# Start of an attention + FFN kernel: first 512 tokens of q and k in two token stages instead of two head halves

## The chip, the cores and the metric

The kernel runs on one core of one Trainium2 chip. The metric is the device time of one execution in microseconds (us), so lower is better. Times inside a trace are counted from the start of the span. "Granted clock" is the clock that the throttle gave the matrix engine, as a share of full speed; the mean over an execution is listed for every run.

The engines are called as in the profile: PE (matmuls and transposes), PEld (its weight loads), DVE (vector engine), ACT (scalar engine), POOL (GpSimd) and SP. A letter q behind a name, as in SPq, means the queue that the engine issues DMAs to. POOLq is served by software and is called the software queue below; SPq and ACTq are hardware queues.

## The reference

```python
# q, k, v: (8, 8, 576, 64) float32: 8 sequences, 8 heads, 576 tokens, head size 64
scores = q @ k.T / sqrt(64)                        # per sequence and head
mask   = (0 <= qpos - kpos) & (qpos - kpos < 64)   # causal window of 64
attn   = softmax(where(mask, scores, -1e9))
x      = (attn @ v).reshape(4608, 512)             # tokens x (heads * 64)
g      = x @ w_gate                                # w_gate, w_val: (512, 1536)
y      = (g * sigmoid(g) * (x @ w_val)) @ w_out    # w_out: (1536, 512)
```

The output is 4608 x 512 float32. Inside, the kernel works in bf16.

## The kernel before

The kernel walks over 36 tiles of 128 tokens. For each tile it transposes q and k (step T), computes scores and exponentials (Sx), multiplies with v and normalises (AV), and transposes the result to xT (X). Four tiles make one FFN block of 512 tokens: twelve steps F (gate and value matmuls for 128 of the 1536 hidden columns each, followed by a tanh on ACT and two operations, uu and hT, on DVE), then the output matmuls. Attention of later tiles is woven between FFN steps, so that PE always has work once the first block runs. The matter is the start, before the first FFN block is under way.

The first 512 tokens of q and k come in four loads, two per tensor, each for four heads. In each load a partition takes four adjacent tokens of a head, 4 x 64 floats, so one run of memory is 1 KB:

```python
def first_loads(self):
    for half in range(2):
        hs = slice(4 * half, 4 * half + 4)
        for eng, dst, src, nm in (("sp", self.fk, self.k, "fk"), ("act", self.fq, self.q, "fq")):
            d = dst[:, hs].rearrange("p h j d -> p h (j d)")
            a = src[0, hs, 0:512, :].rearrange("h (p j) d -> p h (j d)", j=4)
            self.g.op(eng, lambda e, d=d, a=a: e.dma_start(d, a), writes=[(nm, half)], dma=True)
```

All other loads of the start go through the software queue in the order in which they are issued. The order of the start, cut to what matters:

```python
self.first_loads()
self.load_v(0, False)                  # software queue from here
...
for n in range(1, 4):
    self.load_v(n, False)
W(0, 1); W(1, 2)                       # first columns of both FFN weights
...
for f in range(2, 12, 2):
    W(f, f + 2)
...                                    # warm-up matmuls, first casts and transposes
self.Sx(0, 0, True)                    # scores: heads 0-3 of tiles 0-3, then heads 4-7
self.Sx(1, 0, True)
self.first_T("q", 1)
self.Sx(2, 0, True)
self.Sx(3, 0, True)
self.AV(0, 0)
self.Sx(0, 1, True)
...
self.X(1, "act")
self.AV(3, 0)
self.AV(3, 1)
self.F2(0, 0)                          # FFN steps 0 and 1, tokens 0-255
self.X(2, "act")
self.X(3, "act")
self.F2(0, 1)                          # FFN steps 0 and 1, tokens 256-511
load(4)                                # tile 4: q, k, v, behind all W in the queue
load(5)
...
for f in range(2, 6):
    self.F(0, f)
self.T(4)                              # transposes of tile 4, then kT copy on DVE, qz copies on ACT
self.F(0, 6)
self.Sx(4, 0)
self.F(0, 7)
...
```

In T, the copy of k (kT) on DVE must run before the two copies of q (qz) on ACT, and only then can the scores of the tile start.

The softmax here doesn't subtract the row's maximum and nothing guards it: scores larger than these inputs give would overflow.

## Time and profile before

| what | before |
|---|---|
| time, median of 3 runs (lowest to highest) | 350.63 us (350.61 to 350.97) |
| span of the trace, mean granted clock | 348.8 us, 1.0 |
| PE busy | 335.0 us, 96% |
| last of the four first loads lands | 9.67 us |
| v of tile 0 lands | 10.20 us |
| first FFN matmul | 20.86 us |
| FFN step 4 starts | 29.77 us |
| k of tile 4 lands | 33.06 us |
| scores of tile 4 start | 36.23 us |

The first line shown is the busy time of each engine, from the page of the kernel before (busy us, share of the span, number of instructions):

```profile
PE 335.0 (96%) x2385; PEld 175.4 (50%) x2385; DVE 220.4 (63%) x461; ACT 149.2 (43%) x252; POOL 127.3 (37%) x176
```

PE is the engine that bounds the kernel. What is left to win without taking work off PE is its idle time, and that lies mostly at the start. The table of stretches of the kernel before shows it (columns: stretch and its length; busy us and instructions of PE, PEld, DVE, ACT, POOL; granted clock; busy DMA share; GB/s):

```profile
15.00:20.00 5.00, 4.29 (x96) 4.04 (x96) 3.34 (x13) 3.39 (x7) 5.00 (x10) 1.00 1.37 229
20.00:25.00 5.00, 3.19 (x31) 2.58 (x32) 1.28 (x5) 1.28 (x4) 5.00 (x8) 1.00 1.45 196
```

The timeline of PE in the kernel before names the waits (start, busy us, engine, line, operation, out<-in, shape, count, and in brackets the idle time just before and what ended it):

```profile
20.86 0.61 PE L564 MATMUL ps<-xT,Wg 128*128 128x256 bf16 x4 [0.88 <-DVE xb L494]
24.29 0.61 PE L564 MATMUL ps<-xT,Wg 128*128 128x256 bf16 x4 [0.95 <-ACT xT L515]
...
33.23 0.39 PE L411 MATMUL ps<-ident,kn 128*128 128x128 bf16 x4
...
36.23 0.40 PE L454 MATMUL ps<-qz,kT 128*128 128x128 bf16 x4 [0.67 <-ACT qz L419]
```

PE waits 0.88 us for the last normalised attention output before the first FFN half step and 0.95 us for xT before the second halves. The transposes of tile 4 then start at 33.23 us, and its scores wait for a chain that the view of the critical chain spells out (start, length, what):

```profile
33.19 0.70 DVE uu L546
...
33.92 0.69 DVE hT L548
34.61 0.35 DVE kT L416
...
34.98 0.59 ACT qz L417
...
36.23 0.40 PE ps L454 x4
```

The kT copy of tile 4 stands behind hT of FFN step 5 on DVE and so starts at 34.6 us, although its transposes end about 33.8 us. Thus two things hold tile 4 back: DVE's queue, and a DMA, because k of tile 4 lands only at 33.06 us. The view of DMA issues of the kernel before shows the loads of the start and those of tile 4 (out<-in, queue, count, KB each, median us from issue to landing):

```profile
f<-in_k_dram SPq DMA_DIRECT2D x2, 512.0 KB, 6.4
va<-in_v_dram POOLq DMA_DIRECT2D x1, 128.0 KB, 8.9
...
kn<-in_k_dram POOLq DMA_DIRECT2D x2, 64.0 KB, 12.8
```

A load of 64 KB that takes 12.8 us is not slow itself: it stands in the software queue behind weights.

### The profile page before, as it was taken

What the parts mean: (1) busy time and instruction counts of PE and PEld (TensorE: products, weight loads), DVE (VectorE), ACT (ScalarE), POOL (GpSimd) and SP (SyncE); (2) the same over time, 40 slices, a digit from 0 to 9 for tenths busy, and PEclk for the clock granted to TensorE, in tenths of its full rate; (3) what the DMA queues carried; (4) which work ended last, traced back from release to release, by engine and by line L of the source; (5) the groups of instructions that cost most, each with busy time, mean ns of one, the idle gap of its engine ahead of it and who ended that gap; (6) DMA issues with size and microseconds to landing.
All of it is one profiled execution on the core that took longest, in us unless ns stands there. A gap on an engine that the chain in (4) does not pass through costs nothing.

```text
span 348.8 us, 6255 instructions
## 1 busy us (share of the span) xinstructions
PE 335.0 (96%) x2385; PEld 175.4 (50%) x2385; DVE 220.4 (63%) x461; ACT 149.2 (43%) x252; POOL 127.3 (37%) x176
## 2 busy tenths in 40 slices
PE   8779889999999999999999999999999999999996
PEld 3654445554555545555555555555555555444444
DVE  7848583477966665666666666666666666655520
ACT  3643746765544444444444444444444444232321
POOL 8997726835633318233324445334100000000000
PEclk9999999999999999999999999999999999999999
DMA  8999999999989999999999999999945511100012
GB/s 242 188 204 171 218 157 209 201 146 181 141 63 162 148 166 135 150 155 173 137 154 161 169 142 151 159 169 141 160 112 131 94 55 48 59 32 30 30 45 107
DMA packets 177949, 47.93 MB, mean 137 GB/s; under 512 B 160128, under 2 KB 173440, under 8 KB 177920
## 3 DMA queue, kind: packets, MB, share of 16 engines
q0 software_dynamic: 113584, 17.84, 71.4%
q1 hardware_dynamic: 63136, 28.52, 39.8%
q10 hardware_dynamic: 1200, 1.18, 1.0%
q8 instruction: 19, 0.31, 0.4%
q14 instruction: 10, 0.08, 0.1%
HBM read 37.75 MB, written 9.44 MB: 135 GB/s over the span
## 4 chain that ended last, share of the span: by engine, by line
PE 79%; DVE 12%; ACT 5%; DMA 2%; issue 1%
PE ps L538 45%; PE ps L597 23%; PE ps L454 4%; DVE hT L548 3%; DVE uu L546 2%; PE ps L485 2%; PE ps L484 2%; PE ps L357 2%; DMA xT<-xb 2%; DVE xb L494 2%; DVE pt L472 1%; ACT sig L544 1%; ACT qz L419 1%; ACT qz L417 1%; PE ps L564 1%
## 5 line engine op out<-in xcount | busy, mean ns | idle before, releaser
L546 DVE SCALAR_TENSOR_TENSOR uu<-sig,ps 128x512 bf16<-128x512 bf16 x106 | 72.5, 684 | 92.5 <-ACT sig L544 92.2
L538 PE MATMUL ps<-xT,Wg 128*128 128x512 bf16 x424 | 108.8, 379 | 1.0 <-DMA xT<-xb 0.8
L538 PE MATMUL ps<-xT,Wv 128*128 128x512 bf16 x424 | 108.8, 379 | 0.0
L597 PE MATMUL ps<-Wo,hT 128*128 128x512 bf16 x420 | 96.2, 379 | 0.6 <-DVE hT L548 0.6
L544 ACT ACTIVATE sig<-ps 128x512 bf16<-128x512 f32 x106 | 63.3, 597 | 61.5 <-PE ps L538 61.4
L548 DVE SCALAR_TENSOR_TENSOR hT<-uu,ps 128x512 bf16<-128x512 bf16 x106 | 72.8, 686 | 3.7
L538 PEld LDWEIGHTS ps<-xT,Wv 128*128 128x128 bf16 x424 | 41.5, 98 | 50.0 <-DVE hT L583 0.2
L597 PEld LDWEIGHTS ps<-Wo,hT 128*128 128x128 bf16 x420 | 39.8, 98 | 43.5 <-DVE hT L548 0.7
L466 ACT ACTIVATE pt<-ps 128x512 bf16<-128x512 f32 x72 | 42.5, 597 | 43.3 <-PE ps L454 43.2
L538 PEld LDWEIGHTS ps<-xT,Wg 128*128 128x128 bf16 x424 | 39.4, 98 | 41.9 <-DMA xT<-xb 1.3
L371 POOL DMA_DIRECT2D va<-in_v_dram x40 | 34.1, 859 | 66.9 <-PE ps L454 64.9
L288 POOL DMA_DIRECT2D qd<-in_q_dram x54 | 39.0, 734 | 31.6 <-DMA qz<-qd 31.6
L609 ACT ACTIVATE ost<-ps 128x512 f32<-128x512 f32 x35 | 20.9, 597 | 67.1 <-PE ps L597 67.1
L288 POOL DMA_DIRECT2D kn<-in_k_dram x36 | 31.0, 868 | 12.3 <-PE ps L411 11.3
L494 DVE TENSOR_TENSOR xb<-ps,rc 128x256 bf16<-128x256 f32 x72 | 30.5, 424 | 2.5
L454 PE MATMUL ps<-qz,kT 128*128 128x128 bf16 x288 | 28.8, 219 | 3.3 <-ACT qz L419 2.1
L472 DVE TENSOR_TENSOR pt<-pt,mask 128x512 bf16<-128x512 bf16 x64 | 26.6, 415 | 6.3 <-ACT pt L466 6.2
L484 PE MATMUL ps<-vb,pt 128*128 128x65 bf16 x288 | 25.8, 193 | 0.1
L485 PE MATMUL ps<-va,pt 128*128 128x65 bf16 x288 | 25.9, 193 | 0.0
L484 PEld LDWEIGHTS ps<-vb,pt 128*128 128x128 bf16 x288 | 22.0, 98 | 6.7 <-DVE pt L472 0.3
L485 PEld LDWEIGHTS ps<-va,pt 128*128 128x128 bf16 x288 | 19.8, 98 | 6.4
L454 PEld LDWEIGHTS ps<-qz,kT 128*128 128x128 bf16 x288 | 18.7, 97 | 6.6 <-ACT qz L419 3.1
(64 smaller groups left out, 135.1 us busy)
## 6 DMA issues: line engine op xcount, KB each, us to landing
out_dram<-ost SPq DMA_DIRECT2D x35, 256.0 KB, 3.3
vb<-va SPq DMA_DIRECT2D x68, 80.0 KB, 3.4
va<-in_v_dram POOLq DMA_DIRECT2D x32, 128.0 KB, 5.2
kn<-in_k_dram POOLq DMA_DIRECT2D x28, 128.0 KB, 5.8
qd<-in_q_dram POOLq DMA_DIRECT2D x42, 64.0 KB, 4.1
Wo<-in_moe_w_out_dram POOLq DMA_DIRECT2D x2, 768.0 KB, 17.6
Wg<-in_moe_w_gate_dram POOLq DMA_DIRECT2D x5, 256.0 KB, 11.0
Wv<-in_moe_w_val_dram POOLq DMA_DIRECT2D x5, 256.0 KB, 11.6
```

The lines of the kernel that those rows point to most:

```text
L288: self.g.op("pool", lambda e, d=d, a=az: e.dma_start(d, a), writes=kz, dma=True)
L371: g.op("pool", lambda e, d=d, a=a: e.dma_start(d, a), writes=ks, dma=True)
L454: r = e.matmul(sv[:, w, c], self.kT[:, pr, k0:k0 + 128], qz[:, pr, :, 64 * w:64 * w + 64], start=not bias, stop=True)
L466: g.op("act", lambda e: e.activation(po, si, ACTF.Exp, scale=SCALE), reads=[bk], writes=[pk])
L484: e.matmul(av[:, j, :], pt[:, h, 0:128], vb[:, h, 0:65], start=True, stop=False)
L485: r = e.matmul(av[:, j, :], pt[:, h, 64:192], va[:, h, 0:65], start=False, stop=True)
L494: g.op("dve", lambda e: e.tensor_tensor(xo, av[:, :, 0:64], rb, ALU.mult), reads=[bk, ("rc", ir)], writes=[("xb", ix, half)])
L538: r = e.matmul(bank[:, :], W[:, kk, f * 128:f * 128 + 128], xT[:, kk, :], start=(kk == 0), stop=(kk == NK - 1))
L544: g.op("act", lambda e: e.activation(sig[:, :], G[:, :], ACTF.Tanh, scale=0.5), reads=[gk], writes=[("sig", i)])
L546: g.op("dve", lambda e: e.scalar_tensor_tensor(uu[:, :], sig[:, :], 1.0, G[:, :], ALU.add, ALU.mult), reads=[("sig", i), gk], writes=[("uu ...
L548: g.op("dve", lambda e: e.scalar_tensor_tensor(hT[:, f, :], uu[:, :], 0.5, V[:, :], ALU.mult, ALU.mult), reads=[("uu", i), vk], writes=[(" ...
L597: r = e.matmul(OB[:, :], hT[:, f, 128 * u:128 * u + 128], self.Wo[:, f, :], start=(f == 0), stop=(f == NF - 1))
```

## The change

The intent: cut the first 512 tokens by tokens, not by heads. Stage 0 holds tokens 0 to 255 of all heads, so tiles 0 and 1 can be finished whole, including xT. FFN steps 0 to 3 are then run on tokens 0 to 255 first, and these half steps fill PE while tiles 2 and 3 wait for DVE and ACT. A partition of a load now takes two adjacent tokens of a head, so a run of memory is 512 B. The layout of qz changes, so that one copy can write the rows of two tiles. The v loads and two masks move in the issue order of POOL.

The core of the diff (left out: the new layouts of the buffers, the casts, the transposes, and the removal of F2):

```diff
     def first_loads(self):
-        for half in range(2):
-            hs = slice(4 * half, 4 * half + 4)
-            for eng, dst, src, nm in (("sp", self.fk, self.k, "fk"), ("act", self.fq, self.q, "fq")):
-                d = dst[:, hs].rearrange("p h j d -> p h (j d)")
-                a = src[0, hs, 0:512, :].rearrange("h (p j) d -> p h (j d)", j=4)
+        for st in range(2):
+            for eng, dst, src, nm in (("sp", self.fk[st], self.k, "fk"), ("act", self.fq[st], self.q, "fq")):
+                d = dst.rearrange("p h j d -> p h (j d)")
+                a = src[0, :, 256 * st:256 * st + 256, :].rearrange("h (p j) d -> p h (j d)", j=2)
...
-    def F(self, c, f):
+    def F(self, c, f, t0=0, t1=512):
...
-        xk = [("xT", it, u) for u in range(4)]
+        xk = [("xT", it, u) for u in range(t0 // 128, t1 // 128)]
...
-                    r = e.matmul(bank[:, :], W[:, kk, f * 128:f * 128 + 128], xT[:, kk, :],
+                    r = e.matmul(bank[:, 0:n], W[:, kk, f * 128:f * 128 + 128], xT[:, kk, t0:t1],
...
         self.load_v(0, False)
         self.init_pool_a()
+        self.load_v(1, False)
         self.init_mask(self.nmask, "nmask", -30000.0)
-        for n in range(1, 4):
-            self.load_v(n, False)
         W(0, 1)
         W(1, 2)
-        self.init_mask(self.mask, "mask", 0.0)
+        self.load_v(2, False)
+        self.load_v(3, False)
...
+        for half in range(2):
+            for n in range(2):
+                self.Sx(n, half, True)
+        self.first_vb(0, 1, "dve")
         self.first_cast("k", 1)
         self.first_cast("q", 1)
...
+        self.AV(0, 0)
+        self.AV(1, 0)
+        tq = self.first_T("q", 1)
+        self.AV(0, 1)
+        self.AV(1, 1)
...                                    # X(0), X(1), evictions of stage 1
+        self.F(0, 0, 0, 256)
         self.Sx(2, 0, True)
         self.Sx(3, 0, True)
...                                    # rest of attention of tiles 2, 3 between the half steps
+        self.F(0, 3, 0, 256)
+        self.X(3, "act")
...
-        for f in range(2, 6):
+        for f in range(4):
+            self.F(0, f, 256, 512)
+        for f in range(4, 6):
             self.F(0, f)
         self.T(4)
```

## The prediction

> **What bounds the kernel now.** The page shows PE busy 96% of 348.8 us, at full granted clock. The stretches table gives PE 3.10, 4.29 and 3.19 us busy in 10-15, 15-20 and 20-25 us, later mostly over 4.4. The timeline's idle gaps of PE up to the first full FFN step (26.31 us) are 1.17, 1.06, 0.49, 0.88 and 0.95 us, about 4.6 us, ended by DVE's cast, its evictions of q (2 x 0.65 us), xb, and xT. FFN step 4 starts at 29.77 us.
>
> **What the change does.** The same bytes, matmuls and evictions come in another order. Stage 0 (tokens 0-255, all heads) feeds tiles 0 and 1 whole, so attention for them can end early, and four FFN half steps (8 matmuls of 128x256, 0.88 us a step) fill the time while tiles 2 and 3 wait for DVE and ACT. Four warm-up matmuls go. Added: gating ops of 128x256, twice as many, for steps 0 to 3 (684 and 597 ns at 128x512; I estimate 0.42 and 0.41 us), off the critical path. The first loads have 512 B runs in place of 1 KB. "DMA: Bandwidth & Descriptors" (Specifications) of the Trainium skill gives 512 B as the least transfer for line rate; no run here shows these, but the weight loads write 512 B and keep 197 GB/s, so I expect 0.2-0.5 us lost on them.
>
> **Walk through the new order** (estimate, with the trace's durations): first scores at about 9 us (11.5 before); second cast of q at 12 us on ACT, after four exponentials; xT of tiles 0 and 1 at 15.5 and 16.7 us; first FFN half step at 16.7 us (20.86 before); its second halves begin at 25 us; step 4 starts at 28.6 us, 1.2 us sooner.
>
> **What limits the gain.** The software DMA queue is full from 9 to 50 us: each load lands when the one ahead ends, so tile 4's k lands at 33.06 us whatever PE does. The transposes of tile 4 began at 33.23 us, after a 0.2 us wait on that very DMA. In the new kernel PE gets there at about 32 us and must wait: a new wait of about 1.1-1.5 us, `PE ps <- DMA kn`. So the early gain mostly turns into a DMA wait. What passes through is DVE's backlog: before, tile 4's kT copy could begin only at 34.53 us, after hT of step 5, though its transposes ended at 33.84. With PE waiting, DVE is free, and copy, qz and the scores of tile 4 come 0.5-0.9 us sooner (PE idle 0.67 us before those scores goes). After that the order is unchanged, its DMA landings have 2 us of slack, and the lead lasts.
>
> **Prediction:** 350.63 - 0.6 = 350.0 us, 8 in 10 between 349.2 and 351.0. Faster by over 2%: 0.01; within 2%: 0.98; slower by over 2%: 0.01.
>
> **What would show it.** First 128x256 FFN matmul near 16.7 us; full step 4 near 28.6 us; a PE wait on tile 4's kn of 1 us or more ending at 33.1-33.6 us; tile 4's scores near 35.6 us instead of 36.23; then a constant lead of half a microsecond.
>
> **What would make it wrong.** 512 B runs that are much slower than reckoned: then stage 0, and through the queue tile 4, come later, and the gain is nil or negative. The vb copies of tile 2 landing after 20.2 us would stall PE in the middle. If tile 4's loads land sooner, up to 1.3 us is gained.

## More of the kernel before

The DMA view of 6 to 8 us shows what the queues moved while the first loads ran (packets, MB, and the time of the packets as a share of 16 engines):

```profile
q1 hardware_dynamic: 326, 0.33, 55.5%
q10 hardware_dynamic: 300, 0.31, 44.3%
q0 software_dynamic: 198, 0.03, 19.2%
```

Here q1 and q10 carry the first loads (one packet is a run of 1 KB), and q0 is the software queue.

## The result, and the profile after

| what | before | after |
|---|---|---|
| time, median of 4 runs (lowest to highest) | 350.70 us (350.61 to 350.97) | 351.15 us (350.74 to 351.91) |
| last of the four first loads lands | 9.67 us | 11.20 us |
| v of tile 0 lands | 10.20 us | 11.38 us |
| first FFN matmul | 20.86 us | 18.08 us |
| FFN step 4 starts | 29.77 us | 29.95 us |
| k of tile 4 lands | 33.06 us | 34.06 us |
| kT copy of tile 4 starts | 34.53 us | 34.77 us |
| scores of tile 4 start | 36.23 us | 36.47 us |

The ratio of times is 1.0014, with a 95% interval from 0.9996 to 1.0032: not faster, and by the medians 0.45 us slower. A ratio in this text is the mean time of one kernel's fast runs over the mean of the other's fast runs of the same rounds, so it is not quite the ratio of the medians that are quoted beside it (for two kernels below, the runs of before are mostly of earlier rounds; this is said there). All eight of these runs were at full clock.

The busy times of the kernel after, from its page, answer to those of before:

```profile
PE 334.8 (96%) x2397; PEld 176.3 (50%) x2397; DVE 220.4 (63%) x469; ACT 151.3 (43%) x258; POOL 127.4 (36%) x176
```

PE and DVE have the same work as before; ACT has 2 us more. So this is a question of order and waits. The table of stretches of the kernel after:

```profile
15.00:20.00 5.00, 2.91 (x41) 2.35 (x38) 2.82 (x9) 3.96 (x8) 4.87 (x11) 1.00 1.66 196
20.00:25.00 5.00, 4.90 (x77) 4.22 (x74) 3.94 (x13) 3.53 (x8) 5.00 (x7) 1.00 1.39 219
```

From 20 to 25 us PE is busy 4.90 us instead of 3.19, as intended: the half steps fill it. But from 15 to 20 us it is busy only 2.91 us instead of 4.29. The timeline of PE in the kernel after shows where it waits:

```profile
18.08 0.61 PE L536 MATMUL ps<-xT,Wg 128*128 128x256 bf16 x4 [1.35 <-ACT xT L512]
...
26.45 0.61 PE L536 MATMUL ps<-xT,Wg 128*128 128x256 bf16 x4 [0.69 <-ACT xT L512]
...
34.11 0.40 PE L408 MATMUL ps<-ident,kn 128*128 128x128 bf16 x4 [0.54 <-DMA kn<-in_k_dram]
...
36.47 0.40 PE L451 MATMUL ps<-qz,kT 128*128 128x128 bf16 x4
```

The predicted wait on tile 4's k is there, but it ends at 34.1 us, not at 33.1. And the scores of tile 4 follow without a wait of PE, also as predicted. The critical chain of the kernel after says the same: it runs through the DMA, where before it ran through DVE and ACT.

```profile
20.44 13.62 DMA kn<-in_k_dram
...
34.11 0.62 PE ps L408 x8
34.73 1.73 PE ps L536 x8
...
36.47 0.40 PE ps L451 x4
```

But the chain hides a second limit that ends at nearly the same time. The timeline of DVE in the kernel after shows the kT copy directly behind hT of step 5, as before:

```profile
34.10 0.69 DVE L546 SCALAR_TENSOR_TENSOR hT<-uu,ps 128x512 bf16<-128x512 bf16 x1
34.77 0.42 DVE L413 COPY kT<-ps 128x512 bf16<-128x512 bf16 x1
```

So here the prediction failed: DVE was to be free while PE waits, and it was not, because step 5 itself came late.

The load of tile 4's k took 13.7 us in the view of DMA issues of the kernel after, and the loads of the start took longer too:

```profile
fk<-in_k_dram SPq DMA_DIRECT2D x2, 512.0 KB, 7.1
va<-in_v_dram POOLq DMA_DIRECT2D x1, 128.0 KB, 10.1
...
kn<-in_k_dram POOLq DMA_DIRECT2D x2, 64.0 KB, 13.7
```

The DMA view of 6 to 8 us of the kernel after, for comparison with before:

```profile
q1 hardware_dynamic: 631, 0.32, 71.8%
q10 hardware_dynamic: 361, 0.18, 31.5%
q0 software_dynamic: 279, 0.04, 27.0%
```

A packet of 1 KB took 54 ns on q1 and 47 ns on q10 before (55.5% of 16 engines x 2 us over 326 packets, and 44.3% over 300). A packet of 512 B takes 36 and 28 ns after (71.8% over 631, 31.5% over 361): more than half as long for half the bytes. All queues together moved 333 GB/s before and 269 GB/s after in these two microseconds. Note also q0: 279 packets of the software queue got through instead of 198, and these carry little each (0.04 MB).

Last, the timeline of DVE in the kernel after, at the point where the loads of the start are needed:

```profile
11.41 0.52 DVE L314 COPY vb<-va 64x640 bf16<-64x640 bf16 x1 [0.61 <-DMA va<-in_v_dram]
11.94 1.10 DVE L304 CAST ck<-fk 128x1024 bf16<-128x1024 f32 x1
```

DVE stands idle 0.61 us for v of tile 0, and the cast of the second stage of k follows in DVE's order only after it. The same cast took 0.67 us in the first stage and takes 1.10 us here. Why it is slower was not tested.

### The profile page after: what moved, and what is told of

Read it like the earlier page. It is cut to its first block, busy times and chain, and to the rows that moved or that the text cites. A ratio compares the mean times of both kernels' runs of the same rounds, so it can differ in the third digit from the quotient of the medians.

```text
span 350.2 us, 6297 instructions
## 1 busy us (share of the span) xinstructions
PE 334.8 (96%) x2397; PEld 176.3 (50%) x2397; DVE 220.4 (63%) x469; ACT 151.3 (43%) x258; POOL 127.4 (36%) x176
## 4 chain that ended last, share of the span: by engine, by line
PE 70%; DVE 10%; DMA 8%; POOL 5%; ACT 5%; issue 1%; POOLq 0%
PE ps L536 41%; PE ps L560 22%; DMA xT<-xb 4%; DMA kn<-in_k_dram 4%; PE ps L451 3%; DVE hT L546 3%; DVE uu L544 3%; PE ps L482 2%; PE ps L481 2%; ACT sig L542 2%; POOL Wg L390 2%; DVE xb L491 2%; POOL Wv L390 1%; DVE pt L469 1%; ACT qz L416 1%
## 5 line engine op out<-in xcount | busy, mean ns | idle before, releaser
L544 DVE SCALAR_TENSOR_TENSOR uu<-sig,ps 128x512 bf16<-128x512 bf16 (+1 forms) x112 | 74.5, 666 | 98.0 <-ACT sig L542 97.9
L536 PE MATMUL ps<-xT,Wg 128*128 128x512 bf16 (+1 forms) x448 | 111.7, 372 | 3.7 <-ACT xT L512 2.0
L536 PE MATMUL ps<-xT,Wv 128*128 128x512 bf16 (+1 forms) x448 | 111.6, 371 | 0.0
L542 ACT ACTIVATE sig<-ps 128x512 bf16<-128x512 f32 (+1 forms) x112 | 65.2, 582 | 62.7 <-PE ps L536 62.5
L546 DVE SCALAR_TENSOR_TENSOR hT<-uu,ps 128x512 bf16<-128x512 bf16 (+1 forms) x112 | 74.7, 667 | 3.9
L536 PEld LDWEIGHTS ps<-xT,Wv 128*128 128x128 bf16 x448 | 43.8, 98 | 49.4
L536 PEld LDWEIGHTS ps<-xT,Wg 128*128 128x128 bf16 x448 | 41.3, 98 | 44.5 <-DMA xT<-xb 3.3
```

The costliest lines, as they stand in the source:

```text
L536: r = e.matmul(bank[:, 0:n], W[:, kk, f * 128:f * 128 + 128], xT[:, kk, t0:t1], start=(kk == 0), stop=(kk == NK - 1))
L542: g.op("act", lambda e: e.activation(sig[:, 0:n], G[:, 0:n], ACTF.Tanh, scale=0.5), reads=[gk], writes=[("sig", i)])
L544: g.op("dve", lambda e: e.scalar_tensor_tensor(uu[:, 0:n], sig[:, 0:n], 1.0, G[:, 0:n], ALU.add, ALU.mult), reads=[("sig", i), gk], writes ...
L546: g.op("dve", lambda e: e.scalar_tensor_tensor(hT[:, f, t0:t1], uu[:, 0:n], 0.5, V[:, 0:n], ALU.mult, ALU.mult), reads=[("uu", i), vk], wr ...
```

## The experiments

Eighteen kernels ran. Each group of timed runs is compared with runs of the kernel before on the same chip; their medians were 350.62, 350.38, 350.78, 350.77 and 350.59 us in the five groups. The groups ran on four chips: the third and the fourth on the same one, and 11 of the 12 runs of before in the fourth group are those of the third, with one new run of 350.22 us. Everything that ran gave the correct result. The theories:

- **Loads.** The 512 B runs delay the first loads and, through the shared DMA engines, everything in the software queue; this takes back what the new order gains.
- **Order.** The new order gains nothing even with fast loads, because work is moved and not removed.
- **Tile 4.** The order gains, but the wait on tile 4's k eats it; load that earlier and the gain appears.
- **Clock.** PE's idle time at the start makes the throttle take the clock down for a while.
- **Layout.** The new layout of qz slows something later, such as the DMA transposes that write it.

### Is the result stable? Repeats of both kernels

The edit of all three is none: the same sources again.

> The changed kernel itself once more, unchanged, beside the next three on one chip. In its four earlier runs the granted clock was 1.0; in two of six runs of its near twin (tile 4's q and k early) it was 0.995 and those took 353.9 us instead of 351.4. Theory E (the new order leaves PE so little work before its first FFN step that the clock sometimes halves for some microseconds) expects some runs at a granted clock of 0.995 and 2 us or more over the others; theory A alone expects all at 1.0 and 351.0-351.5 us.

Measured with five rounds: median 352.27 us (351.04 to 354.29), ratio 1.0038 with an interval from 1.0011 to 1.0065. So the change is slower by about 0.4%, a little more than the first four runs showed. Four of these six runs had a mean granted clock of 0.995, where all four of the first runs had 1.0 and none of the runs of the kernel before was at 0.995.

> Before, unchanged, one more trace. If the late part is a spread that before has too: the same stamps to within 0.4 us up to 130 us (scores of tile 4 at 35.9-36.4 us), then waits for xT<-xb of another size than the 0.8 us of its first trace (0 to 2 us), at other places. If the waits belong to the change: again 0.8 us or less.

> The changed kernel, unchanged, one more trace. Up to 130 us 0.2 to 0.5 us behind before, as in its other two traces (unless the clock halves near 17 us, which adds up to 1 us); then waits for xT<-xb between 0 and 2 us.

These two were single looks: 350.20 us and 353.13 us, so the two times prove nothing, but the traces show two things. First, the trace of before that the prediction was built on had a chance delay. The timeline of DVE in the first trace of before, and below it in the second:

```profile
13.16 0.68 DVE L314 COPY vb<-va 64x640 bf16<-64x640 bf16 x1
```

```profile
13.13 0.32 DVE L314 COPY vb<-va 64x640 bf16<-64x640 bf16 x1
```

The same copy took 0.36 us longer in the first trace, and everything after it is later by about as much: the first FFN step at 20.86 instead of 20.49 us, the scores of tile 4 at 36.23 instead of 35.85 us. So the typical kernel before reaches the scores of tile 4 at 35.85 us (35.84 and 35.86 in two variants below that leave this part alone). Against that the kernel after, at 36.47 us, is 0.62 us late. In the second trace of before, PE itself waits for the DMA:

```profile
33.26 0.40 PE L411 MATMUL ps<-ident,kn 128*128 128x128 bf16 x4 [0.24 <-DMA kn<-in_k_dram]
```

Second, the third trace of after caught the lower clock. The table of stretches of the third run of after, and below it the same stretch of its first trace:

```profile
19.00:22.40 3.40, 3.40 (x26) 2.88 (x24) 1.01 (x3) 2.09 (x5) 3.40 (x6) 0.50 1.37 234
```

```profile
19.00:22.40 3.40, 3.40 (x60) 3.14 (x58) 2.17 (x6) 2.67 (x7) 3.40 (x6) 1.00 1.36 232
```

The clock is 0.50, from 18.96 to 22.37 us, and PE gets through 26 matmuls instead of 60. Up to there the two traces agree (first half step at 18.11 and 18.08 us); afterwards the scores of tile 4 are at 38.08 us instead of 36.47. One such window of 3.41 us takes half of 3.41/351 off the mean clock, which gives 0.995: the value that the slower runs show. The Trainium skill, "TensorE: Matmul & The Clock Gate" (Part 1, What's actually happening), describes this: the clock falls to one half after an idle window of about 3.4 us and comes back after a busy one, and the window runs freely, so it depends on chance where it falls. The trace agrees in the length and the factor. But PE was not idle for 3.4 us here: its longest single gap before the half step is 1.35 us, with 0.59 and 0.15 us close ahead, and in the 3.41 us before the clock fell it was busy 1.65 us. So a stretch with much idle time was enough in this run; in the first trace of after PE was busy 1.68 us in the same stretch and the clock stayed up.

### Run length by itself

The old order with 512 B runs, at eight loads:

```diff
-                d = dst[:, hs].rearrange("p h j d -> p h (j d)")
-                a = src[0, hs, 0:512, :].rearrange("h (p j) d -> p h (j d)", j=4)
-                self.g.op(eng, ..., writes=[(nm, half)], dma=True)
+                for s in range(2):
+                    d = dst[:, hs, 2 * s:2 * s + 2].rearrange("p h j d -> p h (j d)")
+                    a = src[0, hs, 0:512, :].rearrange("h (p s x) d -> s p h (x d)", s=2, x=2)[s]
+                    self.g.op(eng, ..., writes=[(nm, half, s)], dma=True)
```

> The old order, only the first loads cut into runs of 512 B (eight loads of 256 KB instead of four of 512 KB, everything else as before). Theory A: last of the first loads lands near 11.2 us instead of 9.67, k of tile 4 near 34.0 instead of 33.06, step 4 about 1.3 us later than 29.77, time 0.7 to 1.3 us over before. Rival B: landings within 0.3 us of before, time as before.

Measured: 352.61 us, ratio 1.0055 (1.0018 to 1.0093). The last first load lands at 12.46 us and k of tile 4 at 34.28 us. Two of its six runs had a clock of 0.995 (354.25 and 352.74 us); the other four have a mean of 352.36 us. But this variant also doubles the number of loads, so it needs a control: eight loads with runs of 1 KB.

```diff
+                for s in range(2):
+                    hq = slice(4 * half + 2 * s, 4 * half + 2 * s + 2)
+                    d = dst[:, hq].rearrange("p h j d -> p h (j d)")
+                    a = src[0, hq, 0:512, :].rearrange("h (p j) d -> p h (j d)", j=4)
+                    self.g.op(eng, ..., writes=[(nm, half, s)], dma=True)
```

> Control for the cut of before into 512 B runs, which also had eight first loads instead of four: the old order with eight loads of 256 KB and 1 KB runs. Theory A: landings within 0.4 us of before (last first load near 9.7, k of tile 4 near 33.1), time within 0.4 us of before, so that the 2 us of the 512 B run belong to run length. Rival D (the number of loads costs, not the run length): last first load near 12 us, k of tile 4 near 34.3, time 1.5 to 2 us over before.

Measured: 349.66 us, ratio 0.9973 (0.9941 to 1.0005); last first load at 9.82 us, k of tile 4 at 32.62 us. So the number of loads costs nothing that these runs show. The two kernels differ in the run length, and with it in which tokens or heads a load holds; they ran on two chips, each beside before. The difference is 1.7 us at tile 4's k (34.28 against 32.62), 1.8 us at FFN step 4 (31.20 against 29.40) and about 2.9 us in time (the ratios differ by 0.0082; each was taken against before in its own rounds). The loads of 512 B runs here leave out every second 512 B of memory; those of after do not, and were late too (11.20 us), so that is not what makes them late. The line of tile 4's k in the view of DMA issues, in the kernel with 512 B and below it with 1 KB:

```profile
kn<-in_k_dram POOLq DMA_DIRECT2D x2, 64.0 KB, 13.7
```

```profile
kn<-in_k_dram POOLq DMA_DIRECT2D x2, 64.0 KB, 12.3
```

The loads of q and k were long done when this load was issued, so the delay comes to it through the software queue, in which each load waits for those ahead. The theory of the loads holds in the old order, where nothing else of the change is present. The moved v loads and masks were not tested alone; without them the delay at tile 4's k is as large here (34.28 us) as in after (34.06 us).

In the new order, eight loads of 512 B:

```diff
+                for hh in range(2):
+                    d = dst[:, 4 * hh:4 * hh + 4].rearrange("p h j d -> p h (j d)")
+                    a = src[0, 4 * hh:4 * hh + 4, 256 * st:256 * st + 256, :].rearrange("h (p j) d -> p h (j d)", j=2)
+                    self.g.op(eng, ..., writes=[(nm, st, hh)], dma=True)
```

> The changed kernel with its four first loads cut into eight by heads, runs still 512 B: the partner of the old order with eight loads of 512 B, which took 352.6 us. Theory A says the new order is worth about 1.3 us at equal loads, so near 351.3; rival B says the same as that partner, 352.6.

Measured: 352.04 us, ratio 1.0042 (1.0007 to 1.0077). Here v of tile 0 lands at 8.06 us, so DVE does not wait for it, and the first half step comes at 17.38 us instead of 18.08. Still k of tile 4 lands at 33.93 us, almost as late as in after. And in this trace the clock is at one half from 17.35 to 20.77 us, so that FFN step 4 is at 30.88 us; five of its six runs had a clock of 0.995. In this trace the earlier half step was thus eaten by the clock. The time lies between the two that were expected, and decides between neither.

### Runs of 1 KB in the new order, with loads of 64 partitions

To keep 1 KB runs and the token stages, each load takes only 64 partitions, one for each half of the heads:

```diff
+                for hh in range(2):
+                    d = dst[64 * hh:64 * hh + 64].rearrange("p h j d -> p h (j d)")
+                    a = src[0, 4 * hh:4 * hh + 4, 256 * st:256 * st + 256, :].rearrange("h (p j) d -> p h (j d)", j=4)
```

> The new order with runs of 1 KB in the first loads (four tokens a partition, heads 0-3 on partitions 0-63 and 4-7 on 64-127; same transposes and evictions in number and size; eight loads instead of four). Theory A (the 512 B runs took the gain): the last of the first loads lands near 9.7 us instead of 11.2, v of tile 0 near 10.2 instead of 11.4, k of tile 4 near 33.1 instead of 34.06; full FFN step 4 starts near 28.7 us instead of 29.95; PE then waits about 1 us for tile 4's k; tile 4's scores near 35.6 us; time 0.5 to 0.9 us under before. Rival B (the new order itself gains nothing, run length is not it): step 4 stays at 29.5 us or later, time as before or above.

The same, with q and k of tile 4 loaded ahead of the last weights (`self.load_qk(4)` before the columns 8 to 11):

> Both: 1 KB runs and tile 4's q and k loads ahead of the last four weight loads. Theory A: step 4 starts near 28.7 us, transposes of tile 4 near 32.1 us without a wait, kT copy near 33.5, scores of tile 4 near 35.2 us instead of 36.23, time 0.9 to 1.2 us under before, some 0.3 us better than 1 KB runs alone. Rival B: no better than before.

The premise of both runs failed, that these loads would be about as fast as the old ones. They gave 356.84 and 357.40 us (ratios 1.0165 and 1.0172, intervals 1.0127 to 1.0204 and 1.0133 to 1.0212): the last first load landed at 14.64 and 15.44 us, far later than with 512 B. In these kernels q and k load the same half of the partitions at the same time. The next pair crosses them (`for hh in ((0, 1) if nm == "fk" else (1, 0))`):

> The new order with 1 KB runs once more, where the last one (1 KB runs, each load to 64 partitions, k and q both first to partitions 0-63) spoiled its test: its first loads took until 14.6 us instead of 11.2. Only the order of q's two loads a stage is turned round, so that k fills partitions 0-63 while q fills 64-127 and the reverse. If the slowness was that all loads in flight went to the same half of the partitions, the last of the first loads lands near 9.7-10.3 us. Theory A (run length took the gain) then expects k of tile 4 near 33.1-33.5, step 4 near 28.7-29.2 us, a wait of PE for tile 4's k, scores of tile 4 near 35.6-36.0, time 0.2 to 0.9 us under before. Rival B (the new order itself gains nothing): step 4 at 29.5 us or later and time as before even with the loads landing as in before.

> As the run before with tile 4's q and k loads ahead of the last four weight loads. Theory A: no wait of PE at tile 4's transposes (near 32.2-32.6 us), kT copy of tile 4 at 33.5-33.9 right after step 5's hT, scores of tile 4 at 35.2-35.6, time another 0.3 us less, 0.6 to 1.2 under before. Rival C (DMA wait irrelevant): the same time as the run before.

Measured: 355.53 and 356.32 us (ratios 1.0147 and 1.0157); last first load at 13.36 and 14.09 us. Crossing helps by 1.3 us and no more. The Trainium skill, "SBUF — State Buffer" (Can I just issue two DMAs to hit both halves?), says that two transfers to disjoint partition halves gain next to nothing over one; that crossing left these loads 3.7 us behind the 9.67 us of full-width loads agrees with it in direction. The clock also fell in these four kernels (0.985 to 0.995). They say nothing about run length, since another cost, larger than the one to be tested, came with the edit. They are a failed control, and the cleaner one is the mixed kernel below.

### Is it the wait on tile 4's k?

In the kernel after, q and k of tile 4 are loaded ahead of the last weights:

```diff
         for f in range(2, 12, 2):
+            if f == 8:
+                self.load_qk(4)
             W(f, f + 2)
...
-        load(4)
+        self.load_v(4)
```

> The changed kernel, only tile 4's q and k loads put ahead of the last four weight loads in the software queue. They should land about 5 us sooner (near 29 us), and PE's 0.54 us wait on tile 4's k goes. Theory A says the lead is already lost by then, and DVE's hT of step 5 ends only at 34.8 us, so tile 4's kT copy starts at 34.7-34.8 as in the changed kernel: time within 0.2 us of it. If the DMA wait itself is what costs (rival C), scores of tile 4 come 0.5 us sooner and the time falls by as much.

Measured: 351.60 us, ratio 1.0034 (0.9992 to 1.0076). Tile 4's k lands at 28.57 us, PE's wait of 0.54 us is gone and the transposes start at 33.42 us, 0.7 us sooner. But the scores of tile 4 start at 36.41 us, against 36.47. The critical chain of this kernel shows what holds them now:

```profile
34.11 0.69 DVE hT L546
34.79 0.35 DVE kT L413
...
35.16 0.59 ACT qz L414
```

It is the chain of before: the kT copy behind hT of step 5 on DVE. In after, two limits end within 0.1 us of each other. To take the DMA wait away gained nothing. The theory that the wait on tile 4's k alone eats the gain falls.

### The new order on the old loads

This kernel keeps the old loads (head halves, 1 KB) and the old issue order of the software queue, and runs the new order on them: tiles 0 and 1 first, the FFN half steps between. The stage 1 evictions take the other half of the transposed tokens, and warm-up matmuls fill PE in three places.

```diff
+                d = dst[:, hs].rearrange("p h j d -> p h (j d)")
+                a = src[0, hs, 0:512, :].rearrange("h (p j) d -> p h (j d)", j=4)
...
-        a = tb[ps, prs].rearrange("p c j t -> p c t j")
+        a = tb[ps, :, :, 64 * st:64 * st + 64].rearrange("p c j t -> p c t j")
...
         self.Sx(0, 0, True)
         self.Sx(1, 0, True)
...                                    # cast, transposes, evictions of heads 4-7
         self.Sx(0, 1, True)
         self.Sx(1, 1, True)
...                                    # AV and X of tiles 0 and 1, then as in after
```

> The new order on the old loads: first loads by head halves with 1 KB runs, four of them, v loads and masks in the software queue as in before; only the evictions are cut by tokens, so that tiles 0 and 1 go first, with the four FFN half steps of the change and enough dummy matmuls. Theory A (the loads of the change took its gain): first FFN half step near 17.1 us (before 20.86, changed 18.08), step 4 near 28.9 us (29.77; 29.95), tile 4's k near 33.1 and PE waiting for it 0.5-0.8 us, scores of tile 4 at 35.5-35.8 us, time 0.4 to 0.8 us under before. Rival B (the new order itself gains nothing): step 4 at 29.6 us or later, time within 0.2 us of before or above.

Measured: 350.48 us, ratio 0.9986 (0.9969 to 1.0003), where the kernel after had 352.27 us in the same rounds. The clock was 1.0 or 0.999 in all six runs. v of tile 0 lands at 10.15 us and k of tile 4 at 32.65 us, so the loads are as in before. With the slow loads gone the loss is gone; the warm-up matmuls, which kept the clock up, have a share in that (see the next part). But no gain over before is shown either, though the first FFN half step comes three microseconds sooner. The timeline of PE in this kernel:

```profile
17.44 0.61 PE L537 MATMUL ps<-xT,Wg 128*128 128x256 bf16 x4 [0.69 <-ACT xT L513]
```

FFN step 4 starts at 29.32 us, only 0.1 to 0.45 us before the two traces of before (29.41 and 29.77). Where the three microseconds went is in the timeline of ACT: the xT copy of tile 3, without which the second halves cannot start, in the mixed kernel and below it in the second trace of before (there two copies, of tiles 2 and 3, in one line):

```profile
25.16 0.60 ACT L513 ACTIVATE xT<-ps 128x512 bf16<-128x512 bf16 x1 [0.92 <-PE ps L504]
```

```profile
22.78 1.09 ACT L515 ACTIVATE xT<-ps 128x512 bf16<-128x512 bf16 x2 [3.02 <-PE ps L506]
```

Tile 3's xT is ready at 25.76 us in the new order and at 23.87 us in the old one. The half steps bring their tanh, uu and hT ahead of the attention of tiles 2 and 3 on ACT and DVE, so that attention ends later. PE's idle time of 20 to 25 us is filled with work that was otherwise done after it; what it feeds then starts later. The work was moved. Tile 4 is held by DVE again: hT of step 5 runs from 33.46 us, the kT copy starts behind it at 34.07 us, although PE began the transposes at 32.77 us without a wait for the DMA. So the wait of PE that was to free DVE did not come even with fast loads.

The same with tile 4's q and k loaded early (the edit of above):

> As the run before, with tile 4's q and k loads ahead of the last four weight loads. Theory A: the DMA wait at tile 4's transposes goes, kT copy of tile 4 right behind step 5's hT near 33.8 us, scores of tile 4 near 35.4 us, another 0.1 to 0.4 us less than the run before, 0.6 to 1.1 us under before: the version that beats both. Rival C (the DMA wait is not what limits): same as the run before.

Measured: 350.95 us, ratio 1.0002 (0.9977 to 1.0027). Scores of tile 4 at 35.95 us, against 35.77 without. Again the DMA was not what bound it.

### Is it the clock?

In the kernel after, seven more warm-up matmuls stand in PE's two gaps before the first half step (`self.warm(3, 3)` after the fourth AV, `self.warm(4, 3)` before the first F):

> The changed kernel with seven more dummy matmuls in the two gaps of PE around the transposes of tiles 0 and 1 (three before, four after). Theory E: no run at 0.995, the time is that of the good runs of the changed kernel (351.0-351.4 us), never 353. If the clock plays no part: the same spread as the changed kernel, and the dummies cost nothing or up to 0.3 us.

Measured: 351.44 us, ratio 1.0007 (0.9985 to 1.0028), against 352.27 us of the kernel after in the same rounds. None of its six runs was at 0.995, where after had four. Scores of tile 4 at 36.51 us, as in the first trace of after. So the filled gaps seem to keep the clock up (none of six runs fell, against four of the ten timed runs of after), and that is worth about 0.8 us of the medians here; the counts are small and the intervals of the two ratios overlap, so the size is rough. What remains between this kernel and the mixed one, about 1.0 us of the medians (351.44 against 350.48), is of the size of the delay of the software queue (1.4 us at tile 4's k between these two, 34.09 against 32.65).

### Taking both limits of tile 4 away

The old order with eight loads of 1 KB; tile 4's q and k ahead of the last weights; and tile 4's transposes one FFN step earlier, with its q copies on ACT put behind the next tanh, so that neither hT of step 5 nor the DMA stands before the kT copy:

```diff
-        for f in range(2, 6):
+        for f in range(2, 5):
             self.F(0, f)
-        self.T(4)
+        q_ev = self.T(4, True)         # transposes and kT copy now, q copies returned
+        self.F(0, 5)
+        q_ev()
         self.F(0, 6)
```

> The old order with eight first loads of 1 KB runs, tile 4's q and k ahead of the last four weight loads, and tile 4's transposes one FFN step earlier (kT copy behind step 4's hT, q's evictions behind step 5's tanh). If hT before kT is the limit at tile 4: scores of tile 4 at 35.0-35.2 us without a wait of PE (35.84 with eight loads alone), 0.6 to 1.2 us less than eight loads alone, near 348.8 us. If not, 349.6 us.

Measured: 349.30 us (348.68 to 350.74), ratio 0.9960 (0.9937 to 0.9983): 0.4% below before, with its whole interval below 1, though the 348.8 us that were expected are not reached. Two things weaken this. Eleven of the twelve runs of before in the ratio are of the earlier group on this chip; the one taken beside this kernel had 350.22 us, where the mean of this kernel's six runs is 349.53 us. And eight loads alone gave 0.9973 (0.9941 to 1.0005), so that what the two edits at tile 4 add in time is not shown. What the traces show is the start of the stage. The scores of tile 4 start at 34.79 us, 1.1 us before the typical 35.85, and the critical chain of this kernel runs through PE alone:

```profile
27.38 3.67 PE ps L544 x17
31.05 0.45 PE ps L413 x8
31.50 3.45 PE ps L544 x16
34.95 0.22 PE ps L460 x4
```

The same edits on the mixed kernel:

> The same three edits on the new order with the old loads (and its half steps). Scores of tile 4 at 34.6-34.9 us, 0.4 us before those of the old order with the same edits, time 348.4 us; if the new order is worth nothing once this limit is gone, the same as the old order with these edits.

Measured: 350.27 us, ratio 0.9975 (0.9953 to 0.9997). Scores of tile 4 at 34.96 us. The same old runs of before stand in this ratio, and the mean of these six runs, 350.14 us, is no better than the one run of before beside them. The new order adds nothing to these edits. If anything it is behind: it loses its lead late, as the next part tells.

### The late part, and the layout of qz

Between tile 4 and the end several kernels with the new order lost some more. After 60 us, PE's waits for the DMA transposes of xb into xT sum to 0.8 and 0.3 us in the two traces of before and 0.8 us in the improved old order, but to 1.5, 1.8 and 1.3 us in the three traces of after, 1.1 us in the mixed kernel and 2.4 us in its improved form. One suspect was the layout of qz, which the later DMA transposes also write. Only that layout, in the kernel before:

```diff
-        self.qza = ....rearrange("p (r c e t) -> p r c e t", r=self.NZ, c=4, e=2)
-        self.qz = [self.qza[:, r] for r in range(self.NZ)]
+        self.qza = ....rearrange("p (c e r t) -> p c e r t", r=self.NZ, c=4, e=2)
+        self.qz = [self.qza[:, :, :, r, :] for r in range(self.NZ)]
```

> Before, only the layout of qz changed as in the change (tile index inside instead of outside). Theory Q (the layout slows the DMA transposes and delays xT): up to 130 us as before, then waits of PE for xT<-xb of 1 us and more, time 0.5 to 1 us over before. If the layout is harmless: time within 0.2 us of before.

Measured: 350.83 us, ratio 1.0007 (0.9983 to 1.0031), late waits of 0.9 us, scores of tile 4 at 35.86 us. And the opposite, the old layout in the mixed kernel:

> The new order on the old loads with the old layout of qz (evictions of q still one instruction each). Theory Q: up to 130 us as the run with the new layout (0.4 us ahead of the first trace of before), and the lead is kept: time 0.4 to 0.9 us under before, against 0.3 with the new layout. If the layout is harmless: 0.2 to 0.4 us under before as with the new layout.

Its first run was slow (503.55 us at a clock of 0.656) and carried the profile, so there is no usable trace. Its five fast runs lie between 350.93 and 352.48 us, ratio 1.0023 (1.0000 to 1.0047): no gain from the old layout. The layout theory falls. Why the new order waits somewhat more for late DMA transposes stays open.

### The timed kernels in one table

Left out are the four kernels with loads of 64 partitions, the two of the qz layout and the mixed kernel with tile 4 loaded early; their figures stand above.

| kernel | median us | ratio to before (95%) | k of tile 4 lands | step 4 | scores of tile 4 |
|---|---|---|---|---|---|
| after, first runs | 351.15 | 1.0014 (0.9996 to 1.0032) | 34.06 | 29.95 | 36.47 |
| after, again | 352.27 | 1.0038 (1.0011 to 1.0065) | 34.21 | 30.05 | 36.62 |
| after, warm-ups in the gaps | 351.44 | 1.0007 (0.9985 to 1.0028) | 34.09 | 30.04 | 36.51 |
| after, tile 4 loaded early | 351.60 | 1.0034 (0.9992 to 1.0076) | 28.57 | 29.96 | 36.41 |
| after, eight loads | 352.04 | 1.0042 (1.0007 to 1.0077) | 33.93 | 30.88 | 37.33 |
| old order, eight loads, 512 B | 352.61 | 1.0055 (1.0018 to 1.0093) | 34.28 | 31.20 | 37.65 |
| old order, eight loads, 1 KB | 349.66 | 0.9973 (0.9941 to 1.0005) | 32.62 | 29.40 | 35.84 |
| new order on old loads | 350.48 | 0.9986 (0.9969 to 1.0003) | 32.65 | 29.32 | 35.77 |
| old order, both limits of tile 4 off | 349.30 | 0.9960 (0.9937 to 0.9983) | 27.29 | 29.16 | 34.79 |
| new order on old loads, both limits off | 350.27 | 0.9975 (0.9953 to 0.9997) | 27.97 | 29.33 | 34.96 |

Step 4's start is taken one matmul (0.22 us) ahead of the first record where the trace lacks its first matmul, which is so for about half of these.

## Why the prediction was wrong

The prediction said 350.0 us, with a range of 349.2 to 351.0; the first runs gave 351.15 and the repeat 352.27. It was right that the change moves less than 2%, and wrong in the sign: a small gain was expected and a small loss came.

| step of the prediction | predicted | measured in after | verdict |
|---|---|---|---|
| first loads lose through 512 B runs | 0.2 to 0.5 us | last load +1.5 us, v of tile 0 +1.2 us, tile 4's k +1.0 us | too small, the step that failed |
| first scores | about 9 us | 9.43 us | right, a bit late |
| second cast of q | 12 us | 12.48 us | right, a bit late |
| first FFN half step | 16.7 us | 18.08 us | 1.4 us late |
| from there to step 4 | 11.9 us (16.7 to 28.6) | 11.9 us (18.08 to 29.95) | right |
| wait on tile 4's k | 1.1 to 1.5 us, ends 33.1 to 33.6 | 0.54 us, ends 34.11 | there, other size |
| DVE free for the kT copy, not behind hT of step 5 | yes | no: hT ran 34.10 to 34.79 us, kT copy from 34.77 us | wrong |
| from tile 4's k to its scores | about 2.5 us (33.06 to 35.6) | 2.4 us (34.06 to 36.47) | right |
| lead then kept to the end | constant | some more lost, with the clock and late waits | not quite |

**The step that failed** is, in the words of the prediction, "I expect 0.2-0.5 us lost on them", and with it "tile 4's k lands at 33.06 us whatever PE does". It was argued from the weight loads, which write 512 B and keep 197 GB/s. But those loads run when the first loads are over; the first loads share the DMA engines with each other and with the small packets of v. The prediction cited the Trainium skill, "DMA: Bandwidth & Descriptors" (Specifications), for 512 B as the least transfer at line rate. In this trace 512 B is not as good as 1 KB: 28 to 36 ns a packet against 47 to 54. The four loads have 4096 packets of 512 B instead of 2048 of 1 KB, and at q10's 28 and 47 ns each, 16 engines need 1.2 us more for them ((4096 x 28 - 2048 x 47) ns / 16); with q1's 36 and 54 ns it would be 2.3 us. This is an estimate, and a rough one, since the time of a packet includes waits for those of other queues.

How the queues share the engines fits as well. The same page (Queues, rings and completion order) says that a DMA engine takes the queues in turn, a packet at a time (its packet can hold several of the pieces that the trace counts as packets). From 7 to 9 us in after the three queues moved 447, 447 and 444 packets, as equal turns would have it. From 6 to 8 us they were far from equal (631, 361 and 279), so this holds for a part of the time only. In equal turns a queue with packets half as large gets half the bytes for its turn, while v's packets of 128 B written still get as many turns. That the shorter runs are the cause was shown, in the old order, by the two kernels with eight loads: 1.7 us at tile 4's k and about 2.9 us in time for 512 B against 1 KB. That the cost of a packet and the turns are what makes them late is argued; how the delay divides between the two was not measured.

**A second step failed with it**: "With PE waiting, DVE is free". It rested on step 4 starting 1.2 us sooner; step 4 started at 29.95 us, so hT of step 5 ended at 34.79 us, later than before (34.61), and the kT copy started at 34.77 us, not sooner than 34.53. In the mixed kernel, with fast loads, step 4 came at 29.32 us and not at 28.6, and the kT copy again stood behind hT. So the small predicted gain is not shown even where the first step is mended.

**How it reaches the time.** There are two ways, and they end together. Through the queue, tile 4's k lands 1.0 us later, at 34.06 us, and its scores follow 2.4 us later, as predicted from that landing. Through DVE, v of tile 0 comes late: 0.61 us of waiting for it and 0.4 us of a slower cast, whose cause was not tested, are 1.0 of the 1.4 us by which the first half step is late. In the kernel after with eight loads v of tile 0 came early and the half step 0.70 us sooner, which fits. With the half step late, step 4 comes at 29.95 and not 28.6 us, and hT of step 5 then holds the kT copy too. The run with tile 4 loaded early showed this second limit, at 36.41 us. The remaining 0.4 us of the half step was not traced to a cause.

**What the sum gives.** 350.0 us predicted, plus 0.87 us at tile 4's scores (36.47 against 35.6), is 350.9; 351.15 was measured at full clock. What is left, 0.3 us, is within the spread of runs and of the late waits, which stay open.

**Two smaller errors.** The baseline of the walk was a trace with a chance delay of 0.4 us, so even with the predicted loads the gain at tile 4 would have been 0.25 us (35.85 against 35.6) and not 0.6. The mixed kernel, which has the good loads, agrees: 35.77 us, and a ratio of 0.9986 that does not exclude 1. And the prediction did not think of the clock: PE's thin stretch before the first half step, 2.91 us busy of 5, sometimes costs a window of 3.41 us at half clock. In the repeat the mean clock of four of six runs points to such a window, and of six runs with the gaps filled by warm-up matmuls none does. The prediction's own list of what would make it wrong did name 512 B runs as the first danger, with the right consequence; it gave that too little weight.

## What to carry to other kernels

Before cutting a load differently, look at the size of its runs and at what shares the DMA engines with it: a shorter run costs not only the load itself but, through a queue that is full, every load behind it (here more than 20 us later). Filling idle time of the busiest engine gains nothing by itself when the work put there makes its helpers deliver the next piece later; ask for the piece whose arrival ends the last wait. Where two limits end within a tenth of a microsecond, remove both in one kernel before judging either. Here the DMA wait alone gave nothing; the DVE limit alone was not tried; both together, with eight loads, brought tile 4's scores 1.1 us forward and measured 0.4% less, of which the share of the two edits is open.

## What the Trainium skill lacked or had wrong

- "DMA: Bandwidth & Descriptors" (Specifications) gives 512 B as the least transfer for line rate, which by itself would let one expect no loss. Here 512 B runs were clearly slower than 1 KB runs: 28 to 36 ns a packet against 47 to 54 ns, 269 against 333 GB/s from 6 to 8 us, and 352.61 against 349.66 us for two kernels with eight loads (on two chips, ratios to before 1.0055 and 0.9973).
- The same page (Queues, rings and completion order) names the turns of the queues, but not what follows for queues with unlike packets. Here three busy queues moved 447, 447 and 444 of the packets that the trace counts in 2 us (but 631, 361 and 279 in a stretch that overlaps it), so the one with 128 B written per packet moved as many as those with 512 B.
- "SBUF — State Buffer" (The DMA setup-cost knee) advises the largest single transfer. Cutting 512 KB loads into 256 KB loads at the same run length showed no cost here: last landing 9.82 against 9.67 us, tile 4's k at 32.62 against 33.06 us, and 349.66 us in time.
- "TensorE: Matmul & The Clock Gate" (Part 1) speaks of an idle window of about 3.4 us before the clock halves, but gives no share of idle time at which a window counts as idle. Here the half-clock window, 3.41 us long, came after gaps of at most 1.35 us each, with PE busy 1.65 us of the 3.41 us before it.
